# The second MLP product of the last two batches by seven products instead of eight

## The chip, the cores and the metric

The kernel runs on one core of a Trainium2 chip. The metric is the device time of one execution, in microseconds (us), as the median of several runs. A core has TensorE (PE in the profile; its weight loads are PEld), VectorE (DVE), ScalarE (ACT), GpSimd (POOL) and SyncE (SP, which here only issues transfers). Each engine takes its instructions in the order in which they are written and waits for the others by semaphores.

## The reference, cut to what matters

```python
# 8 batches, 12 heads, 448 positions, 64 columns per head
q_n, k_n = rmsnorm(q, g_q), rmsnorm(k, g_k)
attn = softmax(q_n @ k_n.T / 8) @ v                  # per batch and head
x = attn, heads side by side                         # 3584 tokens x 768
h = x @ w_in                                         # 3584 x 2048
g = maximum(h, 0) + alpha * minimum(h, 0)
out = g @ w_out                                      # 3584 x 768, float32
```

The change concerns the last line, for the last two of the eight batches (896 of the 3584 tokens).

## The kernel before, in words

Attention goes by groups of two head pairs; the MLP of a batch is laid beside the attention of the next batch, by a planner (L639 to L715) that gives each unit of MLP work a cost (`UP`, 1.13, and `DOWN`, 2.6) and deals the units out over the gaps between bursts of attention. The order on every engine is written out by this Python code; nothing reorders it later.

There are two kinds of MLP unit. `up` (L473) makes one 128-row slice of `g`, transposed, for one batch: six matmuls of 128x448 into a PSUM bank, then ScalarE writes `ah`, the product scaled by alpha (L494), then VectorE takes the maximum of product and `ah` into `gT` (L498). `gT` (L91) holds 16 such slices, f16, with 896 token columns: the even batch of a pair in columns 0 to 447, the odd one behind it. `down` (L500) makes 128 tokens by 384 of the 768 output columns: 16 matmuls of 128x384, one for each slice of `gT`, then VectorE copies the bank to `osb` (L520), and two transfers, issued by SP, write it out (L528). A pair of batches has seven token tiles `t` (0 to 6) and two column halves `oh`.

PSUM has eight banks: the pool `pss` has two tiles of two banks (tag `sc`, for attention scores), `psa` has one tile of two banks (tag `acc`), `psf` has two single banks (tag `mm`). `up` and `down` take a bank from `psf` in turn, or, with `spare` set, from `psa` (`bank`, L442). In the profile their tiles are `hT` and `op` in `psf`, `hTa` and `opa` in `psa`. A bank is free again when VectorE has read it (L498 or L520).

The end of the program is the list `rest` (L704 to L710, run at L917): the 16 `up` units of the last batch (7), with one of five `down` units left from before (token tile 0, half 1; tiles 1 and 2, both halves) ahead of every third `up`, and then the eight `down` units of token tiles 3 to 6. Every third entry of `rest` has `spare` set. The last `down` is done in two parts of 192 columns (L503), so that the copy and the transfers of the first part lie beside the second.

GpSimd computes squares (L155) and the scaled q and k (L179), issues the loads of v and of the weights, and adds up the softmax denominators of some head groups (`add_up`, L356). Its last work in the program is `add_up` for the last head group (23). `w_out_sb` (L90) holds the whole second weight matrix, f16, as 16 slices of 128 rows by 768 columns.

Of the kernel before, what the change touches and what calls it, by code (L numbers as in the profile page):

```python
# [9 lines left out]
FP32 = mybir.dt.float32  # L10
FP16 = mybir.dt.float16
# [10 lines left out]
def kernel(  # L22
# [12 lines left out]
    nc = tc.nc  # L35

    B, H, S, D = q.shape
    DM = H * D
    DF = moe_w_in.shape[1]
    J = S // 64  # L40
# [3 lines left out]
    NF = DF // 128  # L44
    OH = DM // 2
# [4 lines left out]
    EB = 3  # L50
# [5 lines left out]
    ld = ctx.enter_context(tc.tile_pool(name="ld", bufs=2))  # L56
    att = ctx.enter_context(tc.tile_pool(name="att", bufs=2))
    ffn = ctx.enter_context(tc.tile_pool(name="ffn", bufs=2))
    pss = ctx.enter_context(tc.tile_pool(name="pss", bufs=2, space=bass.MemoryType.PSUM))
    psa = ctx.enter_context(tc.tile_pool(name="psa", bufs=1, space=bass.MemoryType.PSUM))  # L60
    psf = ctx.enter_context(tc.tile_pool(name="psf", bufs=2, space=bass.MemoryType.PSUM))
# [7 lines left out]
    out4 = out.rearrange("(b p j) m -> b j p m", b=B, j=J)  # L69
# [16 lines left out]
    cols = cst.tile([128, NF + 2], FP32, name="cols", tag="cols")  # L86
# [3 lines left out]
    w_out_sb = cst.tile([128, NF, DM], FP16, name="w_out_sb", tag="w_out_sb")  # L90
    gT = cst.tile([128, NF, W], FP16, name="gT", tag="gT")  # L91
# [4 lines left out]
    nat, sqs, qs, ss_t, rr_t, qkT, vt, xT = {}, {}, {}, {}, {}, {}, {}, {}  # L96
# [220 lines left out]
    expT, rden, scs = {}, {}, {}  # L317

    def pre(ys):
        return len(ys) == 1 and ys[0] >= PRE and ys[0] % G == G - 1  # L320
# [179 lines left out]
    def down(b0, t, oh, jobs=(), spare=False):  # L500
# [24 lines left out]
        for c in range(parts):  # L525
            for half in range(2):
# [3 lines left out]
                    in_=o[ds(64 * half, 64), ts(c, PW)],  # L530
                )

    def spin(count, wide=True):

        ps = psf.tile([128, 512], FP32, name="spin", tag="mm")
        for _ in range(count):
            nc.tensor.matmul(
                out=ps[:, :S], lhsT=idle32[:, :128] if wide else ident,
                rhs=idle32 if wide else idle, start=True, stop=True,
            )  # L540
# [5 lines left out]
    den_at, av_at, split = {}, {}, {}  # L546
# [4 lines left out]
    m = 0  # L551
    while m < NG * J or steps:
        n = len(bursts)
# [20 lines left out]
        while len(bursts[n]) < limit and m < NG * J:  # L574
            y, j = divmod(m, J)
# [10 lines left out]
    NB = len(bursts)  # L586
# [17 lines left out]
    jobs = {}  # L604
    for y in range(G, NG):

        early = y < G + 2
        if early:
            n = turn_at[y - 1] + 1
        elif y == G + 2:  # L610
            n = den_at[G - 1]
        elif y == 2 * G:
            n = turn_at[y] - 4
        elif y % G == 1:
            n = den_at[y - 4] - 1 - pre((y - 2,))
        elif y % G:
            n = den_at[y - G] - pre((y - G,))
        else:
            n = av_at[y - 4]
# [22 lines left out]
    for b in range(B):  # L642
        ups = [(UP / 3 if b == 0 and ft < 4 else UP, up, (b, ft)) for ft in range(NF)]
        odd = b % 2
        new = [
            (DOWN, down, (b - odd, t, oh))
            for t in (range(3, J) if odd else range(3)) for oh in range(2)
        ]
# [16 lines left out]
    first = av_at[G - 1]  # L665
    gaps = [[] for _ in range(NB)]
    for b in range(B - 1):
        lo, hi = av_at[G * b + G - 1], av_at[G * b + 2 * G - 1]
        ups, old, new = (list(u) for u in periods[b])
        mlp = sum(u[0] for u in ups + old + new)  # L670
        stop = hi
# [5 lines left out]
        for n in range(lo, hi):  # L677
            clock += cost(n)
            free = True
            while ups or old or new:  # L680
                two = n in dens and pre(dens[n]) and len(gaps[n]) < 2
                if old and (not ups or (free or two) and (
                    wide(n) or len(old) > sum(wide(c) for c in range(n, hi))
                )):
                    u = old.pop(0)
                elif ups:
                    u = ups.pop(0)
                else:
                    u = new.pop(0)
# [12 lines left out]
                if n < hi - 1 and not short and clock + ahead > per * (n - lo + 1):  # L702
                    break
    ups, old, new = periods[B - 1]  # L704
    rest = []
    for n, u in enumerate(ups):
        if n % 3 == 0 and old:
            rest.append(old.pop(0)[1:])
        rest.append(u[1:])
    rest += [u[1:] for u in old + new]  # L710

    for n in range(1, NB):

# [7 lines left out]
    for n, g in enumerate((g_q, g_k)):  # L721
        for h in range(2):
            nc.gpsimd.dma_start(
                out=rows[NF + n : NF + n + 1, ds(64 * h, 64)], in_=g.unsqueeze(0)
            )
    load_qk(1, True)
    load_qk(2)

    spin(2)
    spin(17, False)  # L730
    ct = psf.tile([128, 512], FP32, name="ct", tag="mm")
    nc.tensor.transpose(ct[:, : NF + 2], rows, ident32[: NF + 2, : NF + 2])
# [4 lines left out]
    for h in range(2):  # L737
# [13 lines left out]
        out=gain, in0=cols[:, NF : NF + 1], in1=cols[:, NF + 1 : NF + 2]  # L751
# [30 lines left out]
    for n in range(NB):  # L782
# [6 lines left out]
        for t in first_tiles:  # L789
            if t == (0, J - 2):  # L790
                spin(1)
            elif t == (1, J - 3):
                spin(2, False)
            elif t == (1, J - 2):
                spin(1, False)
            elif t == (0, J - 1):
                turn_one(1, "q")
            elif t == (1, 0):
                turn_one(1, "k")
            elif t == (1, J - 1):  # L800
                turn(2)
            score(*t)
            if n == den_at[G - 1] - 1 and t == tiles[-1]:
                begin(0)
                begin(1)
            elif lead and t == tiles[0]:
                soft(*t)
                den(dens[n])
                attv(avs[n], 0, True, (log, invert))
            elif lead and t == tiles[1]:  # L810
                begin(2)
# [32 lines left out]
        if n in roots:  # L844
            y = roots[n]
# [41 lines left out]
        for k, (f, a) in enumerate(gaps[n]):  # L887
# [3 lines left out]
            else:  # L891
                f(*a, spare)
                done += 1
                if n in jobs and not (lead and done < 5) and (
                    n < av_at[2 * G - 1] or done % 2
                ):
                    g, c = jobs[n].pop(0)
# [3 lines left out]
                while late and done == late[0][0]:  # L901
                    _, g, c = late.pop(0)
# [11 lines left out]
                add_up(y, j)  # L914
        for f, a in jobs.pop(n, []) + post.get(n, []):
            f(*a)
    for k, (f, a) in enumerate(rest):  # L917
        f(*a, spare=k % 3 == 2)


# [28 lines left out]
```

## Time and profile before

| what | value |
|---|---|
| median of three runs | 428.4 us (428.13 to 429.29) |
| span of the profiled execution, first to last instruction | 425.6 us (no other time of it is given; the median lies 2.8 us above it) |
| TensorE busy | 413.7 us (97%) |
| ScalarE, GpSimd, VectorE busy | 275.3, 239.4 and 222.4 us |
| granted TensorE clock | 1.000 of full speed |
| last 16 `up` units begin | 372.40 us after the span's start |
| last matmul ends | 421.81 us |

A profile is one execution, recorded on the chip. The chain of waits follows the work that ended last back to what released each step. The timeline gives instructions in order of time: start and duration in us, engine, line, operation, output and inputs with their sizes, the count when several are merged, and in brackets the idle time before it with what ended it. Matmuls are pipelined; in the timeline their recorded durations overlap by some 0.16 us, in the chain of waits they do not.

### The profile page before, as it was taken

The page shows a single profiled execution, that of the slowest core. Times are in us where ns is not written, and L with a number is a line of the kernel's source. Part 1 is how long each engine was busy: PE and PEld are TensorE (multiplying, and loading weights), DVE is VectorE, ACT ScalarE, POOL GpSimd, SP SyncE. Part 2 cuts the span into 40 slices and gives each one's busy share as a digit, 9 for nine tenths or more (in the row PEclk, how much of TensorE's full clock was granted, in tenths as well). Part 3 has the DMA queues.
Part 4 walks back from the last instruction along what each step waited for, and adds up shares of the span by engine and source line. Part 5 has one row for each costly group of instructions (what it writes and reads, how often), then busy time and mean ns, then how long its engine had stood idle before and what let it go on. Part 6 is the DMA issues. An engine that isn't in the chain of part 4 may idle for free.

```text
span 425.6 us, 11138 instructions
## 1 busy us (share of the span) xinstructions
PE 413.7 (97%) x4755; PEld 216.5 (51%) x4755; DVE 222.4 (52%) x331; ACT 275.3 (65%) x384; POOL 239.4 (56%) x173
## 2 busy tenths in 40 slices
PE   7889999999999999999999999999999999999996
PEld 3344454544455454544555545554555445555554
DVE  4875964456454636636564545647453343343421
ACT  5898887778856686578846677668847575332200
POOL 6789993494997299373984479482973009000000
PEclk9999999999999999999999999999999999999999
DMA  8999999999538965568455963545333500111033
GB/s 199 242 240 224 204 195 204 204 195 238 117 73 131 210 102 126 85 158 168 97 104 109 187 148 106 105 103 126 62 55 85 104 2 22 39 37 39 18 76 75
DMA packets 68529, 53.36 MB, mean 125 GB/s; under 512 B 35568, under 2 KB 68480, under 8 KB 68480
## 3 DMA queue, kind: packets, MB, share of 16 engines
q1 hardware_dynamic: 53680, 39.73, 42.5%
q0 software_dynamic: 13984, 11.81, 18.5%
q10 hardware_dynamic: 816, 1.11, 1.0%
q8 instruction: 37, 0.61, 0.6%
q14 instruction: 12, 0.10, 0.1%
HBM read 45.62 MB, written 11.01 MB: 133 GB/s over the span
## 4 chain that ended last, share of the span: by engine, by line
PE 86%; ACT 5%; DVE 4%; POOL 2%; issue 1%; ACTq 1%; POOLq 0%
PE op L508 29%; PE hT L454 21%; PE hTa L454 9%; PE sc L329 8%; PE opa L508 6%; PE av L368 5%; PE dn L368 3%; ACT expT L343 2%; PE avb L368 2%; PE dnb L389 2%; ACT ah L494 2%; DVE gT L498 1%; POOL sq L155 1%; DVE ss L163 1%; ACTq L108 1%
## 5 line engine op out<-in xcount | busy, mean ns | idle before, releaser
L343 ACT ACTIVATE expT<-sc,expb 128x896 f16<-128x896 f32 x168 | 161.3, 1003 | 42.8 <-PE sc L329 42.6
L508 PE MATMUL op<-w_out_sb,gT 128*128 128x384 f16 (+1 forms) x752 | 125.8, 323 | 0.5 <-DVE gT L498 0.5
L508 PEld LDWEIGHTS <-gT 128*128 128x128 f16 x912 | 86.0, 98 | 64.7 <-issue 11.8
L454 PE MATMUL hT<-xT,w_in_sb 128*128 128x448 f16 x552 | 114.7, 353 | 0.8 <-DVE gT L498 0.5
L179 POOL TENSOR_TENSOR qs<-nat,rr 128x896 f16<-128x896 f32 x41 | 68.4, 1690 | 82.4 <-issue 45.6
L454 PEld LDWEIGHTS <-w_in_sb 128*128 128x128 f16 x768 | 73.2, 98 | 73.8 <-issue 9.4
L494 ACT ACTIVATE ah<-hT,cols 128x448 f16<-128x448 f32 x91 | 57.4, 632 | 46.5 <-PE hT L454 45.6
L498 DVE TENSOR_TENSOR gT<-hT,ah 128x448 f16<-128x448 f32 x92 | 57.3, 623 | 50.7 <-ACT ah L494 49.8
L155 POOL TENSOR_TENSOR sq<-nat 128x896 f32<-128x896 f32 (+1 forms) x47 | 75.5, 1625 | 7.9 <-DMA nat<-in_q_dram 7.3
L520 DVE COPY osb<-op 128x384 f32<-128x384 f32 (+1 forms) x47 | 25.7, 548 | 69.3 <-PE op L508 68.9
L329 PE MATMUL sc<-qT,kT 64*32 64x448 f16 (+1 forms) x1092 | 54.0, 356 | 4.4 <-ACT expT L343 2.2
L356 POOL TENSOR_TENSOR rden<-rden,expT 128x896 f32<-128x896 f32 x30 | 56.8, 1895 | 2.4
L163 DVE TENSOR_REDUCE ss<-sq 128x14 f32<-128x896 f32 (+1 forms) x48 | 48.9, 1039 | 1.9 <-POOL sq L155 1.8
L454 PE MATMUL hTa<-xT,w_in_sb 128*128 128x448 f16 x204 | 44.1, 352 | 0.0
L494 ACT ACTIVATE ah<-hTa,cols 128x448 f16<-128x448 f32 x34 | 21.6, 634 | 21.0 <-PE hTa L454 20.9
L329 PEld LDWEIGHTS <-kT 64*32 64x32 f16 (+1 forms) x1092 | 17.0, 93 | 35.7 <-issue 29.3
L498 DVE TENSOR_TENSOR gT<-hTa,ah 128x448 f16<-128x448 f32 x34 | 21.2, 624 | 19.6 <-ACT ah L494 18.9
L439 DVE TENSOR_TENSOR xT<-av,rden 128x896 f16<-128x896 f32 x16 | 17.5, 1091 | 21.5 <-ACT rden L410 15.4
L368 PEld LDWEIGHTS <-vt 64*32 64x32 f16 (+1 forms) x1260 | 21.4, 94 | 12.7 <-issue 2.5
L508 PE MATMUL opa<-w_out_sb,gT 128*128 128x384 f16 x160 | 27.7, 326 | 0.0
L368 PE MATMUL av<-expT,vt 64*32 64x448 f16 (+1 forms) x812 | 26.6, 349 | 0.0
L356 POOL TENSOR_TENSOR rden<-expT 128x896 f32<-128x896 f16 x6 | 11.3, 1878 | 20.9 <-ACT expT L343 20.9
(67 smaller groups left out, 215.8 us busy)
## 6 DMA issues: line engine op xcount, KB each, us to landing
out_dram<-osb SPq DMA_DIRECT2D x109, 96.0 KB, 2.2
nat<-in_q_dram SPq DMA_DIRECT2D x46, 224.0 KB, 4.3
nat<-in_k_dram SPq DMA_DIRECT2D x46, 224.0 KB, 4.8
vt<-in_v_dram POOLq DMA_DIRECT2D x16, 336.0 KB, 5.9
w_in_sb<-in_moe_w_in_dram POOLq DMA_DIRECT2D x12, 256.0 KB, 7.2
w_out_sb<-in_moe_w_out_dram POOLq DMA_DIRECT2D x4, 768.0 KB, 11.1
nat<-in_q_dram ACTq DMA_DIRECT2D x2, 224.0 KB, 4.3
nat<-in_k_dram ACTq DMA_DIRECT2D x2, 224.0 KB, 5.7
```

Source lines behind the costliest of these rows:

```text
L155: nc.gpsimd.tensor_mul(out=sqf[:, c], in0=src[:, c], in1=src[:, c])
L163: nc.vector.tensor_reduce(out=o[:, c], in_=sqs[y, nm][:, c], axis=AXIS_X, op=ALU.add)
L179: eng.tensor_mul(out=t.rearrange("p j h d -> p h j d"), in0=nat[y, nm], in1=rr_t[y][:, "qk".index(nm)].unsqueeze(3).broadcast_to((128, 2, ...
L329: nc.tensor.matmul(out=sc[ds(64 * g + m * c, m), par, :S].rearrange("p (j c) -> p j c", j=J), lhsT=kT[ds(64 * par, 64), j, g, ts(c, m)], r ...
L343: nc.scalar.activation(out=expT[y][:, j], in_=scs[y, j][:, :, :S], func=AF.Exp, scale=QK_SCALE, bias=expb[:, 0:1],)
L356: nc.gpsimd.tensor_add(out=s, in0=e[:, 0] if j == 1 else s, in1=e[:, j])
L368: nc.tensor.matmul(out=accs[g][ds(m * h, m), :S], lhsT=weights(g, y, par, ts(c, m), j), rhs=expT[y][ds(64 * g, 64), j, par, :], start=(j = ...
L454: nc.tensor.matmul(out=hT[:, :S], lhsT=w_in_sb[:, g * G + i, ts(ft, 128)], rhs=xT[b][:, g, i, :], start=(i == 0 and g == 0), stop=(i == G ...
L494: nc.scalar.activation(out=ah, in_=hT[:, :S], func=AF.Copy, scale=alpha_sb[:, ft : ft + 1])
L498: nc.vector.tensor_max(out=gT[:, ft, ds((b & 1) * S, S)], in0=hT[:, :S], in1=ah)
L508: nc.tensor.matmul(out=ops[c][:, :PW], lhsT=gT[:, ft, ts(t, 128)], rhs=w_out_sb[:, ft, ds(oh * OH + c * PW, PW)], start=(ft == 0), stop=(f ...
L520: nc.vector.tensor_copy(out=o[:, ts(c, PW)], in_=ops[c][:, :PW])
```

## The change

The four `down` units of tiles 1 and 2, and the eight of tiles 3 to 6, leave `rest`; only the one of tile 0 stays there, at its head. Behind `rest` come three calls of `quad`, for tiles (1, 2), (3, 4) and (5, 6). A `quad` makes both tiles and both column halves, four blocks of 128x384. The four blocks are products of a 2x2 block matrix of `gT` (two token tiles by two halves of the 16 slices) with a 2x2 block matrix of the weights (two halves of the slices by two column halves). By a Strassen scheme that takes seven block products, of eight matmuls each, in place of eight.

- `mix_weights` makes four sums of weight blocks, `tw[0]` to `tw[3]`, each 128x3072 f16, on GpSimd, in the order 0, 2, 1, 3. It stands at the end of step `NB - 2` of the main loop, behind the `add_up` of the last head group in GpSimd's order. The sums lie in buffers of `expT` that head groups 21 and 22 held.
- `mix` makes four sums of `gT` blocks, `gs`, each 128x1024 f16, on VectorE. For tiles 1 and 2 they are put into `rest`, one behind each of the entries 2, 5, 8 and 11; for the next `quad` they are put among the VectorE work of the one before.
- In a `quad` the seven products go into four PSUM banks (three of them twice; `quad` 1 and 3 use `pss`, `quad` 2 uses `psf` and `psa`). Three products per `quad` are copied or finished by ScalarE, four by VectorE additions, and one addition is on GpSimd; the outputs leave by `send`. In the last `quad` the last product is done in two parts of 192 columns.

```diff
+    halves = (slice(0, NF // 2), slice(NF // 2, NF))
+    tw, mixes = {}, {}
+    def mix_weights():
+        w = {(f, m): w_out_sb[:, halves[f], ts(m, OH)] for f in range(2) for m in range(2)}
+        for n in range(2):
+            t = att.tile([128, 2, NF // 2, OH], FP16, name="tw", tag="expT", bufs=EB)
+            tw[2 * n], tw[2 * n + 1] = t[:, 0], t[:, 1]
+        for n, x, y in (
+            (0, w[0, 1], w[0, 0]), (2, w[1, 1], w[0, 1]), (1, w[1, 1], tw[0]), (3, w[1, 0], tw[1])
+        ):
+            nc.gpsimd.tensor_sub(out=tw[n], in0=x, in1=y)
+    def mix(t0, eng):
+        a = {(n, f): gT[:, halves[f], ts(t0 + n, 128)] for n in range(2) for f in range(2)}
+        new = [
+            ld.tile([128, NF // 2, 128], FP16, name="gs", tag="nat", bufs=6) for _ in range(4)
+        ]
+        mixes[t0] = new
+        return [
+            lambda f=f, o=o, x=x, y=y: f(out=o, in0=x, in1=y)
+            for f, o, x, y in (
+                (eng.tensor_add, new[0], a[1, 0], a[1, 1]),
+                (eng.tensor_sub, new[1], new[0], a[0, 0]),
+                (eng.tensor_sub, new[2], a[0, 0], a[1, 0]),
+                (eng.tensor_sub, new[3], a[0, 1], new[1]),
+            )
+        ]
+    def send(b0, t, oh, o, c=slice(0, None), split=False):
...
+    def quad(b0, t0, wide, last=False, jobs=()):
+        a = {(n, f): gT[:, halves[f], ts(t0 + n, 128)] for n in range(2) for f in range(2)}
+        w = {(f, m): w_out_sb[:, halves[f], ts(m, OH)] for f in range(2) for m in range(2)}
+        s1, s2, s3, s4 = mixes[t0]
...
+        def product(bank, g, v, first, cols=slice(0, OH)):
+            for f in range(NF // 2):
+                nc.tensor.matmul(
+                    out=bank[:, cols], lhsT=g[:, f, :], rhs=v[:, f, cols],
+                    start=(first and f == 0), stop=(f == NF // 2 - 1),
+                    skip_group_check=True,
+                )
...
+        product(x, a[0, 0], w[0, 0], True)
+        m1 = part("m1")
+        nc.scalar.copy(out=m1, in_=x)
+        product(y, s2, tw[1], True)
+        u2 = part("u2")
+        nc.vector.tensor_add(out=u2, in0=y, in1=m1)
+        job()
+        product(p, s1, tw[0], True)
+        m5 = part("m5")
+        nc.scalar.copy(out=m5, in_=p)
+        product(q, s3, tw[2], True)
+        u3 = part("u3")
+        nc.vector.tensor_add(out=u3, in0=q, in1=u2)
+        job()
+        product(x, a[0, 1], w[1, 0], False)
+        o = ffn.tile([128, OH], FP32, name="osb", tag="osb", bufs=4)
+        nc.scalar.copy(out=o, in_=x)
+        send(b0, t0, 0, o)
+        nc.gpsimd.tensor_add(out=u3, in0=u3, in1=m5)
+        send(b0, t0 + 1, 1, u3)
+        job()
+        product(p, s4, w[1, 1], False)
+        o = ffn.tile([128, OH], FP32, name="osb", tag="osb", bufs=4)
+        nc.vector.tensor_add(out=o, in0=p, in1=u2)
+        send(b0, t0, 1, o)
+        job()
+        for c in (slice(0, OH // 2), slice(OH // 2, OH)) if last else (slice(0, OH),):
+            product(q, a[1, 1], tw[3], False, c)
+            nc.vector.tensor_add(out=u2[:, c], in0=q[:, c], in1=u2[:, c])
+            send(b0, t0 + 1, 0, u2, c, last)
...
     ups, old, new = periods[B - 1]
+    old = [u for u in old if u[2][1] == 0]
     rest = []
     for n, u in enumerate(ups):
         if n % 3 == 0 and old:
             rest.append(old.pop(0)[1:])
         rest.append(u[1:])
-    rest += [u[1:] for u in old + new]
...
+        if n == NB - 2:
+            mix_weights()
+    mixing = mix(1, nc.vector)
     for k, (f, a) in enumerate(rest):
         f(*a, spare=k % 3 == 2)
+        if k in (2, 5, 8, 11):
+            mixing[k // 3]()
+    nexts = {1: mix(3, nc.vector), 3: mix(5, nc.vector)}
+    for t in (1, 3, 5):
+        quad(B - 2, t, t != 3, t == 5, nexts.get(t, ()))
```

More of the change, by code (lines that the diff above doesn't have):

```diff
@@ new lines, in send, with job, part @@
+    def send(b0, t, oh, o, c=slice(0, None), split=False):
+        for half in range(2):
+            bb, j = divmod(2 * t + half, J)
+            dst = out4[b0 + bb, j, :, ts(oh, OH)]
+            (nc.scalar if split and half else nc.sync).dma_start(
+                out=dst[:, c], in_=o[ds(64 * half, 64), c]
+            )
[3 more added lines that the diff above has]
+        s1, s2, s3, s4 = mixes[t0]
+        if wide:
+            pairs = [pss.tile([128, 2, 512], FP32, name="oq", tag="sc") for _ in range(2)]
+            x, y, p, q = (t[:, n, :OH] for t in pairs for n in range(2))
+        else:
+            x = psf.tile([128, 512], FP32, name="oq", tag="mm")[:, :OH]
+            y = psf.tile([128, 512], FP32, name="oq", tag="mm")[:, :OH]
+            t = psa.tile([128, 2, 512], FP32, name="oqa", tag="acc")
+            p, q = t[:, 0, :OH], t[:, 1, :OH]
+        def product(bank, g, v, first, cols=slice(0, OH)):
[4 more added lines that the diff above has]
+                    skip_group_check=True,
+                )
+        jobs = iter(jobs)
+        def job():
+            for f in jobs:
+                f()
+                break
+        def part(name):
+            return ld.tile([128, OH], FP32, name=name, tag="sq", bufs=4)
+        product(x, a[0, 0], w[0, 0], True)
[28 more added lines that the diff above has]
+            send(b0, t0 + 1, 0, u2, c, last)
```

## The prediction, made before the changed kernel was run

> **What bounds the kernel now.** I read the page's summary first, then the end of the chain of waits, then the timeline of each engine over the last 75 us, since nothing ahead of 362 us moves: the built order of all engines is the same up to the new GpSimd instructions.
>
> ```profile
> span 425.6 us, 11138 instructions
> PE 413.7 (97%) x4755; PEld 216.5 (51%) x4755; DVE 222.4 (52%) x331; ACT 275.3 (65%) x384; POOL 239.4 (56%) x173
> PEclk9999999999999999999999999999999999999999
> ```
>
> TensorE is busy for 97% of the span at full clock. At the end it is the only bound:
>
> ```profile
> 413.96 2.60 PE opa L508 x16
> 416.56 5.25 PE op L508 x48
> 421.81 0.02 issue
> 421.84 0.36 DVE osb L520
> ```
>
> A `down` takes 2.60 us for 16 matmuls, 0.1626 us each; behind the last come a copy of 0.36 us and 3.4 us of transfer until 425.6. The stretch that changes is this (timeline of TensorE, then of VectorE, then of GpSimd):
>
> ```profile
> 372.24 1.30 PE L454 MATMUL hT<-xT,w_in_sb 128*128 128x448 f16 x6
> 373.37 1.30 PE L454 MATMUL hTa<-xT,w_in_sb 128*128 128x448 f16 x6
> 374.51 1.30 PE L454 MATMUL hT<-xT,w_in_sb 128*128 128x448 f16 x6
> ...
> 374.24 0.62 DVE L498 TENSOR_TENSOR gT<-hT,ah 128x448 f16<-128x448 f32 x1 [0.95 <-ACT ah L494]
> 375.37 0.63 DVE L498 TENSOR_TENSOR gT<-hTa,ah 128x448 f16<-128x448 f32 x1 [0.51 <-ACT ah L494]
> ...
> 352.43 9.79 POOL L356 TENSOR_TENSOR rden<-rden,expT 128x896 f32<-128x896 f32 x5
> ```
>
> An `up` takes 1.135 us (372.40, 373.54, 374.67 by the chain). VectorE releases its bank about 1.5 us after its last matmul, and three banks rotate, so 0.7 us of slack is left when `up` units follow each other. GpSimd is free from 362.22.
>
> One more view decides the case: what VectorE and GpSimd do to each other when both use SBUF. VectorE's in-place scaling of k takes 0.44 us at best and up to 1.90 us:
>
> ```profile
> 110.97 1.88 POOL L356 TENSOR_TENSOR rden<-expT 128x896 f32<-128x896 f16 x1
> ...
> 111.98 1.12 DVE L288 TENSOR_SCALAR kT<-kT,gain 128x896 f16<-128x896 f16 x1
> ...
> 122.69 3.46 POOL L155 TENSOR_TENSOR sq<-nat 128x896 f32<-128x896 f32 x2
> ...
> 122.93 1.69 DVE L288 TENSOR_SCALAR kT<-kT,gain 128x896 f16<-128x896 f16 x1
> ...
> 28.41 1.09 DVE L179 TENSOR_TENSOR qs<-nat,rr 128x896 f16<-128x896 f32 x1 [0.64 <-DMA nat<-in_q_dram]
> ...
> 29.26 1.79 POOL L179 TENSOR_TENSOR qs<-nat,rr 128x896 f16<-128x896 f32 x1
> ```
>
> The one at 111.98 ends at 113.10, 0.25 us after the GpSimd instruction that ran meanwhile (110.97 to 112.85). The one at 122.93 ends at 124.62, 0.25 us after the first of the two squares (122.69 to 124.37). It does not share; it waits for the whole GpSimd instruction, and then goes ahead of GpSimd's next, which loses 0.14 us (3.46 against 3.32 for an undisturbed pair). The last two rows are the only place where GpSimd starts under a VectorE instruction with two SBUF inputs: 1.79 us is the longest of 41 such instructions (median 1.69). So that form of VectorE instruction holds GpSimd up too. The new `gs` sums have this form. The maxima (L498) and the copies (L520) have at most one SBUF input beside PSUM, and keep 0.62 and 0.56 us whatever GpSimd does.
>
> [...]
>
> **Part by part.**
>
> *Removed and added on TensorE.* Twelve `down` units (192 matmuls' worth) become 3 x 7 x 8 = 168: 24 x 0.1626 = **-3.9 us**. Their drains lie beside the next product: per `quad` of 9.1 us, ScalarE gets three copies (nearest row: `ah`, 0.63) and VectorE four additions (0.6) and four sums; each bank has at least two products (2.6 us) before its reuse. So nothing there.
>
> *Sums of weights.* No row has 3072 elements. The nearest is the add of two f16 inputs, 1.878 us for 896. The squares give a fixed part: 0.925 for 448 and 1.69 for 896, so 0.16 fixed. Then (1.878 - 0.16) / 896 x 3072 + 0.16 = **6.05 us** each. Bounds: 5.41 by the squares' slope (1.708 ns), 6.50 with the add's 1.895 in proportion. All four go back to back from 362.3: `tw[0]` to 368.4, `tw[2]` to 374.4, `tw[1]` to 380.45, `tw[3]` to 386.5. The first `quad` needs `tw[1]` at 391.9, so the sums themselves are in time, by 11 us.
>
> *Sums of `gT`.* f16 in, f16 out, 1024 elements: 0.62 us for 896 (the f16 copies of q) gives 0.69; the f32 form (1.09 for 896) gives 1.2 as upper bound. Alone they cost nothing: 1.87 + 0.69 of VectorE in three `up` units of 3.41 us, and one delay of 0.69 against 0.7 us of slack.
>
> *The new wait.* They are not alone: GpSimd is busy without a gap from 362 to 386, and the first two `gs` stand there, with the maxima that free TensorE's banks queued behind them.
> 1. VectorE reaches `gs` 1 behind the second maximum, at 376.0. `tw[1]` (374.4 to 380.45) holds it. It ends at 380.45 + 0.5 = 380.95 (0.5: 0.69 less the 0.19 that the waiting instructions above had behind them).
> 2. The third maximum runs until 381.6. TensorE has done `up` 4 and 5 and stands from 378.07, since `up` 6 takes the bank of `up` 3. It goes on at 381.65: **3.6 us** lost.
> 3. `tw[3]` starts at 380.95 and ends at 387.0. The maxima of `up` 4 and 5 end at 382.8; `gs` 2 then waits until 387.0 and ends at 387.5; the maximum of `up` 6 at 388.1. TensorE does `up` 6 to 8 until 385.05 and stands until 388.2, for `up` 9: **3.15 us**.
> 4. `gs` 3 and 4 meet an idle GpSimd: nothing. Of a sum's length d the loss is about 4d - 17.5: 4.1 us at 5.41, 6.7 at 6.05, 8.5 at 6.50.
>
> So **+6.7 us**. Were the wait not there, no other work would be late: TensorE would run on.
>
> [...]
>
> *The end.* Last copy and transfers are as before, but four outputs (0.79 MB) leave in the last 2.5 us instead of two. In this kernel's tail they moved at 150 to 174 GB/s in busy slices and the queues went up to 242 GB/s early. Between 0 and 1.0 us; I take **+0.4**.
>
> **Sum**, on the profiled execution: 425.6 - 3.9 + 6.7 + 0.4 = 428.8 of span; the median lies 2.8 above the span, so **431.6 us**.
>
> **The rivals.**
>
> *No exclusion for this form.* VectorE's two-input sums could read beside GpSimd; the rows show only the one-input form waiting. Then the two stalls vanish: 428.4 - 3.9 + 0.4 = **424.9**, faster (424.4 to 425.5). For it: no VectorE instruction with two SBUF inputs starts under a GpSimd instruction in this trace. Against: the 1.79 row.
>
> *Short sums of weights.* With the squares' slope the stalls shrink to 4.1 us: 428.4 - 3.9 + 4.1 + 0.4 = **429.0**; below 5.65 us a sum it counts as no change or nearly. For it: squares of the same shape are shorter than adds. Against: both f16 rows are adds, and take 1.88.
>
> *GpSimd keeps the port.* If GpSimd's next instruction goes ahead of the waiting `gs` 1, VectorE waits until 386.5 once, and TensorE from 378.07 to 387.7: 9.6 us, **434.5**. At 218.65 a waiting instruction came just behind a GpSimd start and took 1.90 us, one instruction, not two; so unlikely.
>
> *The change doesn't do what it says*: excluded as far as the built order goes, which has 32 matmuls fewer (the split parts count double).
>
> **How the numbers follow.** Two stalls of 3 us or so each: 0.62 (430.0 to 434). Short sums: 0.11. No exclusion: 0.23. GpSimd first: 0.04. A measurement tells 0.3%, 1.3 us, from no change, so faster (under 427.1) 0.23, within 0.10, slower 0.67. The range must reach to the second case, 424.4, and takes the upper price of a sum and of the tail (8.5 and 1.0): 434.0, and 434.5 with the last rival. The likeliest case's own range is 429.0 to 434.0.
>
> **What would show it.** Right: `gs` 1 and 2 of some 4.5 us instead of 0.7, each ending 0.5 us behind a `tw`; TensorE idle before `up` 6 and `up` 9, for 3 us or so each, released by VectorE L498; a TensorE sum 3.9 us shorter; no stall in the `quad`s. Wrong: `gs` all of 0.7 us with `tw` beside them, or `tw` much off 6 us, or TensorE waiting inside a `quad`.

## The result, and the profile after

The changed kernel takes 437.29 us (median of 5 runs, 437.03 to 438.31) against 428.13 us in the same session: a ratio of 1.0221 (the two medians alone give 1.0214), with a 95% interval of 1.0202 to 1.0239. It is 9.2 us slower. The forecast was 431.6 us, with 434.5 us as the upper end: slower was right, the size was not.

The profiled execution took 438.31 us, the longest of the five; its span is 436.2 us, that of the other four 435.3. These lines of its page answer to those shown of before:

```profile
span 436.2 us, 11110 instructions
PE 412.1 (94%) x4723; PEld 213.5 (49%) x4723; DVE 238.8 (55%) x343; ACT 280.1 (64%) x393; POOL 267.5 (61%) x180
PE   7889999999999999999999999999999999778884
PEclk9899999999999999999999999999999999999999
```

TensorE has less to do (412.1 against 413.7 us) and is no longer busy without a break: from slice 35 on the digits are 7 and 8 (the 4 at the end holds the last transfer). The next two views show two different kinds of gap. First the part with the 16 `up` units, by the timeline of TensorE, VectorE and GpSimd:

```profile
377.46 1.30 PE L454 MATMUL hTa<-xT,w_in_sb 128*128 128x448 f16 x6
381.93 2.43 PE L454 MATMUL hT<-xT,w_in_sb 128*128 128x448 f16 x12 [3.17 <-DVE gT L498]
...
388.32 2.43 PE L454 MATMUL hT<-xT,w_in_sb 128*128 128x448 f16 x12 [2.83 <-DVE gT L498]
...
376.60 4.74 DVE L555 TENSOR_TENSOR gs<-gT 128x1024 f16<-128x1024 f16 x1
381.26 1.14 DVE L498 TENSOR_TENSOR gT<-hT,ah 128x448 f16<-128x448 f32 x2
382.33 0.61 DVE L498 TENSOR_TENSOR gT<-hTa,ah 128x448 f16<-128x448 f32 x1
382.86 4.88 DVE L555 TENSOR_TENSOR gs<-gs,gT 128x1024 f16<-128x1024 f16 x1
...
389.26 0.68 DVE L555 TENSOR_TENSOR gs<-gT 128x1024 f16<-128x1024 f16 x1
...
362.86 11.98 POOL L545 TENSOR_TENSOR tw<-w_out_sb 128x3072 f16<-128x3072 f16 x2
374.80 12.38 POOL L545 TENSOR_TENSOR tw<-w_out_sb,tw 128x3072 f16<-128x3072 f16 x2
```

This is the forecast wait. The first two `gs` take 4.74 and 4.88 us beside `tw`; the third, with GpSimd idle, takes 0.68. The maxima between them (one input in PSUM, one in SBUF) keep their 0.6 us with `tw[3]` beside them. TensorE stands twice, for 3.17 and 2.83 us, each time until a maximum behind a `gs` has released a bank.

Then the part with the seven products, first `quad`, with the two ScalarE copies and the VectorE addition that end the three gaps:

```profile
397.40 1.46 PE L588 MATMUL oq<-w_out_sb,gT 128*128 128x384 f16 x8
399.43 2.77 PE L588 MATMUL oq<-tw,gs 128*128 128x384 f16 x16 [0.57 <-ACT m L606]
402.78 1.46 PE L588 MATMUL oq<-tw,gs 128*128 128x384 f16 x8 [0.57 <-ACT m L613]
...
407.49 1.47 PE L588 MATMUL oq<-tw,gT 128*128 128x384 f16 x8 [0.65 <-DVE osb L627]
...
398.90 0.48 ACT L606 COPY m<-oq 128x384 f32<-128x384 f32 x1 [0.67 <-PE oq L588]
402.25 0.48 ACT L613 COPY m<-oq 128x384 f32<-128x384 f32 x1 [2.87 <-PE oq L588]
...
406.87 0.56 DVE L627 TENSOR_TENSOR osb<-oq,u 128x384 f32<-128x384 f32 x1
```

The second product goes into another bank than the first and takes nothing that the copy `m1` makes. Yet it starts only when that copy (398.90 to 399.38) has ended. The fourth product (402.78) starts in the same way behind the copy at 402.25, the last (407.49) behind the addition at 406.87. In this `quad` the banks `x` and `y` are two halves of one two-bank tile, and so are `p` and `q`; each of the three gaps lies where TensorE goes on to the second bank of a tile whose first bank is still being read.

From these views the 10.6 us between the two spans (436.2 and 425.6) come out as follows.

| stage | how it is read | us |
|---|---|---|
| up to the first of the 16 units | begins at 373.08 against 372.40 by the chains; not the change, see below | +0.7 |
| matmuls removed | 24 x 0.1626 | -3.9 |
| 16 `up` units | 373.08 to 397.56, 24.5 against 18.2 | +6.3 |
| three `quad`s | 397.56 to 431.68, 34.1 against 27.3 | +6.8 |
| last matmul to the end | 4.5 against 3.8 | +0.7 |

The first row belongs to this execution. Its granted clock is 0.83 between 10 and 20 us, where that of before is 1.00. By the timelines the units begin at 372.92 to 373.09 in three of the ten profiles of this case, this one among them, and at 372.03 to 372.25 in the other seven, five of which are of kernels with the same code up to there.

### The profile page after: what moved, and what is told of

Read it like the earlier page. It is cut to its first block, busy times and chain, and to the rows that moved or that the text cites. A ratio compares the mean times of both kernels' runs of the same rounds, so it can differ in the third digit from the quotient of the medians.

```text
span 436.2 us, 11110 instructions
## 1 busy us (share of the span) xinstructions
PE 412.1 (94%) x4723; PEld 213.5 (49%) x4723; DVE 238.8 (55%) x343; ACT 280.1 (64%) x393; POOL 267.5 (61%) x180
## 4 chain that ended last, share of the span: by engine, by line
PE 82%; DVE 8%; ACT 6%; issue 1%; POOL 1%; ACTq 1%; DVEq 0%; POOLq 0%
PE op L508 23%; PE hT L454 20%; PE sc L329 8%; PE hTa L454 8%; PE av L368 5%; PE oq L588 4%; PE opa L508 4%; DVE gs L555 3%; PE dn L368 3%; PE avb L368 2%; ACT expT L343 2%; DVE gT L498 2%; ACT ah L494 2%; PE dnb L389 2%; PE oqa L588 1%
## 5 line engine op out<-in xcount | busy, mean ns | idle before, releaser
L508 PE MATMUL op<-w_out_sb,gT 128*128 128x384 f16 x592 | 101.4, 326 | 0.5 <-DVE gT L498 0.5
L508 PEld LDWEIGHTS <-gT 128*128 128x128 f16 x704 | 66.1, 98 | 53.0 <-issue 11.8
L498 DVE TENSOR_TENSOR gT<-hT,ah 128x448 f16<-128x448 f32 x93 | 57.7, 623 | 46.9 <-ACT ah L494 46.1
L520 DVE COPY osb<-op 128x384 f32<-128x384 f32 x37 | 20.5, 556 | 55.0 <-PE op L508 54.6
L454 PE MATMUL hTa<-xT,w_in_sb 128*128 128x448 f16 x198 | 42.8, 352 | 0.0
L622 POOL TENSOR_TENSOR u<-u,m 128x384 f32<-128x384 f32 x3 | 3.7, 1249 | 37.1 <-DVE u L616 37.1
```

The source lines that it names most:

```text
L454: nc.tensor.matmul(out=hT[:, :S], lhsT=w_in_sb[:, g * G + i, ts(ft, 128)], rhs=xT[b][:, g, i, :], start=(i == 0 and g == 0), stop=(i == G ...
L498: nc.vector.tensor_max(out=gT[:, ft, ds((b & 1) * S, S)], in0=hT[:, :S], in1=ah)
L508: nc.tensor.matmul(out=ops[c][:, :PW], lhsT=gT[:, ft, ts(t, 128)], rhs=w_out_sb[:, ft, ds(oh * OH + c * PW, PW)], start=(ft == 0), stop=(f ...
```

## The experiments

All ratios are to the kernel before, in the same session and on the same chip; its medians are 428.1 us beside the change, 427.3 beside `no_weight_sums`, `sends` and the two kernels named `both_sends`, and 427.5 beside the others.

| kernel | us | ratio, 95% interval |
|---|---|---|
| the change | 437.29 | 1.0221 (1.0202 to 1.0239) |
| own_tiles | 431.98 | 1.0099 (1.0086 to 1.0112) |
| late_sums | 431.08 | 1.0080 (1.0067 to 1.0093) |
| half_weights | 432.00 | 1.0106 (1.0090 to 1.0123) |
| no_weight_sums | 431.06 | 1.0081 (1.0066 to 1.0096) |
| both | 426.13 | 0.9961 (0.9949 to 0.9974) |
| sends | 436.67 | 1.0223 (1.0206 to 1.0240) |
| both_sends | 424.05 | 0.9922 (0.9910 to 0.9934) |
| both_sends_whole | 424.44 | 0.9933 (0.9917 to 0.9949) |

**own_tiles: each bank from a tile of its own.**

```diff
-        if wide:
-            pairs = [pss.tile([128, 2, 512], FP32, name="oq", tag="sc") for _ in range(2)]
-            x, y, p, q = (t[:, n, :OH] for t in pairs for n in range(2))
...
+        x, p = (
+            pss.tile([128, 2, 512], FP32, name="oq", tag="sc")[:, 0, :OH] for _ in range(2)
+        )
+        y = psf.tile([128, 512], FP32, name="oqf", tag="mm")[:, :OH]
+        q = psa.tile([128, 2, 512], FP32, name="oqa", tag="acc")[:, 0, :OH]
```

> The changed kernel, with the four PSUM banks of each block product group taken from four tiles (the first bank of two tiles of two banks, one single bank, the first bank of the third two-bank tile) in place of two banks of one tile. Theory A: two banks of one tile are waited for as one, so that TensorE, before the second, fourth and last product, waits for the ScalarE copy or VectorE addition that reads the neighbouring bank; those nine waits cost 6.8 us in the profile (34.1 us from the first to the last matmul of this part against 27.3), of which only the one between the two halves of the last product (0.6) is a bank of its own: 437.3 - 6.2 = 431.1 us, and no TensorE idle time in this part but that one. Rival B: TensorE waits because the copies and additions themselves come too late: the waits stay, 437 us.

Measured: 431.98 us. The waits of TensorE from 370 us on, with the total, the number and the longest:

```profile
PE hT L454 <- DVE gT L498: 4.3, 2, 3.2
PE oqa L585 <- DVE u L629: 0.4, 1, 0.4
```

Of the nine waits in the `quad`s (three, two and three, and the one between the halves of the last product) eight are gone; the one between the halves, inside one bank, stays. The copies and additions take as long as before (0.48 and 0.56 us). So theory A holds: the waits were for neighbouring banks of a shared tile, not for late copies. The edit also takes the banks from other pools, but the built order names the sharing: in the changed kernel the first matmul of the first `quad`'s fourth product carries a wait for ScalarE, with separate tiles it carries none. It is a wait in the program, not one that the chip makes. From the first to the last matmul the `quad`s take 27.9 us (396.72 to 424.66) in place of 34.1, 6.2 less; the time fell by 1.22% (5.2 us). Of the difference 0.6 us was given back at the end (5.1 us behind the last matmul in place of 4.5), which is taken up below. (The two stalls among the `up` units sum to 4.3 us here and to 6.0 in the changed kernel, but the 16 units take 24.5 us in both: between the stalls twelve matmuls took 4.11 us in place of 2.43, see the account of the prediction.)

**late_sums, no_weight_sums and half_weights: what the first sums of `gT` wait for.** `late_sums` moves them behind GpSimd's work:

```diff
-        if k in (2, 5, 8, 11):
-            mixing[k // 3]()
+        if k > 12:
+            mixing[k - 13]()
```

> The changed kernel, with the first four VectorE sums of gT put behind entries 13 to 16 of the list in place of 2, 5, 8 and 11, when GpSimd has ended its sums of weights. Theory A: VectorE's two-input sums wait for the GpSimd instruction that runs, and the maxima behind them hold TensorE up, 6.3 us in all: each sum takes 0.7 us, TensorE has no idle time among the 16 first-product units, 437.3 - 6.0 = 431.3 us. Rival B: a sum between the maxima is by itself more than VectorE's slack; the stall moves along with the sums: 435 us or more.

`no_weight_sums` keeps their place and takes GpSimd's work away. It leaves out the sums of weights and puts plain weight blocks in their place, so its output is not the product:

```diff
-            tw[2 * n], tw[2 * n + 1] = t[:, 0], t[:, 1]
...
-            nc.gpsimd.tensor_sub(out=tw[n], in0=x, in1=y)
+        tw.update({0: w[0, 1], 2: w[1, 1], 1: w[1, 1], 3: w[1, 0]})
```

> The changed kernel with the four sums of weights on GpSimd left out (plain weight blocks of the same shape in their place), and the sums of gT on VectorE where they were, at entries 2, 5, 8 and 11. Theory A: without a GpSimd instruction beside them all four sums take 0.7 us and TensorE does not stand among the 16 units: the 6.3 us go, 431 us. Rival B: the place of the sums alone holds the maxima up: TensorE still waits before units 6 and 9, 435 us or more.

`half_weights` keeps both, and cuts each GpSimd instruction in two:

```diff
-            nc.gpsimd.tensor_sub(out=tw[n], in0=x, in1=y)
+            for c in (slice(0, 4), slice(4, 8)):
+                nc.gpsimd.tensor_sub(out=tw[n][:, c], in0=x[:, c], in1=y[:, c])
```

> The changed kernel, with each of the four GpSimd sums of weights in two instructions of half the size (about 3.1 us each). Theory A: VectorE waits for the rest of the one GpSimd instruction that runs, then goes first: the first two sums of gT take 2 to 2.5 us in place of 4.7 and 4.9, TensorE loses 1 to 2 us in place of 6.3: 432.5 us. Rival B: GpSimd keeps its access as long as it has work: the sums wait until GpSimd ends at 387, 440 us. Rival C: both share one rate, each is stretched: nothing changes, 437 us.

Measured: 431.08, 431.06 and 432.00 us. The VectorE sums in the timelines, first of `no_weight_sums`:

```profile
376.77 0.68 DVE L549 TENSOR_TENSOR gs<-gT 128x1024 f16<-128x1024 f16 x1
380.18 0.68 DVE L549 TENSOR_TENSOR gs<-gs,gT 128x1024 f16<-128x1024 f16 x1
```

and then of `half_weights`, with its GpSimd rows:

```profile
375.71 2.13 DVE L556 TENSOR_TENSOR gs<-gT 128x1024 f16<-128x1024 f16 x1
379.36 1.98 DVE L556 TENSOR_TENSOR gs<-gs,gT 128x1024 f16<-128x1024 f16 x1
383.24 1.60 DVE L556 TENSOR_TENSOR gs<-gT 128x1024 f16<-128x1024 f16 x1
386.73 1.60 DVE L556 TENSOR_TENSOR gs<-gT,gs 128x1024 f16<-128x1024 f16 x1
...
361.98 12.26 POOL L546 TENSOR_TENSOR tw<-w_out_sb 128x1536 f16<-128x1536 f16 x4
374.19 13.60 POOL L546 TENSOR_TENSOR tw<-w_out_sb,tw 128x1536 f16<-128x1536 f16 x4
```

At the same place among the maxima a sum takes 0.68 us without GpSimd, and TensorE has no wait among the 16 units, so the place alone costs nothing. With GpSimd instructions of 3.1 us in place of 6, the wait is at most the rest of one of them, and the waiting VectorE instruction goes in between: GpSimd's second group of four takes 13.60 us, 1.34 more than the first. TensorE's single wait among the `up` units is then 0.56 us, and the 16 units take 19.2 us against the 18.2 of 16 x 1.135. Sharing at a common rate would have changed nothing, and GpSimd keeping its access would have made it worse; both fall. So, in these runs, a VectorE sum with two SBUF inputs waits for the whole GpSimd instruction that is running, and then goes ahead of GpSimd's next. (The other direction is seen in the last section.)

**both: separate tiles and late sums.**

> Both edits together. Theory A: the two losses lie one behind the other and add up: 437.3 - 6.2 - 6.0 = 425.1 us, under the kernel before (428.1) by the 3.9 us of 24 matmuls less what the end gives back. Rival B: a new wait takes the place of those removed, as the sums then lie closer to their use: 428 us or more.

Measured: 426.13 us, 0.39% under the kernel before. The two losses add up: 1.22% and 1.41% alone, 2.60% together. TensorE goes from the first `up` (373.24, the 373.08 of its timeline and the overlap of 0.16) to the last matmul (419.35) in 46.1 us, against 49.4 before: 3.9 less, and 0.6 for the wait between the halves. But of this gain of 3.3 us only some 1.7 (0.39%) arrives; 1.4 go at the end. From VectorE's last addition (ended at 419.74) to the span's end there are 4.8 us, against 3.4 before. SP's timeline shows where they are (each row is two issues of one output):

```profile
416.65 1.12 SPq L568 DMA_DIRECT2D out_dram<-osb  x2
417.87 1.37 SPq L568 DMA_DIRECT2D out_dram<-u  x2
419.34 1.28 SPq L568 DMA_DIRECT2D out_dram<-osb  x2
420.71 1.19 SPq L568 DMA_DIRECT2D out_dram<-u  x2
```

An issue takes SP some 0.6 us. The four outputs become ready between 416.53 and 419.74, and SP is issuing all but without a break from 416.65 to 421.90 (eight issues, not the ten of the next expectation); its share of the first half of the last output, ready at 418.47, is not issued until 420.71. (A row of the last output is one issue of each half; ScalarE gives out the other two.)

**both_sends, both_sends_whole and sends: the end.** `send` has an argument that gives one of an output's two transfers to ScalarE; before, only the last output used it.

```diff
-        send(b0, t0, 0, o)
+        send(b0, t0, 0, o, split=last)
...
-        send(b0, t0 + 1, 1, u3)
+        send(b0, t0 + 1, 1, u3, split=last)
...
-        send(b0, t0, 1, o)
+        send(b0, t0, 1, o, split=last)
```

> The kernel with both edits (four tiles for the banks, late sums), and in the last group of products one of the two transfers of every output issued by ScalarE, in place of all but the last on SP. Theory A: behind the last matmul (419.35 us in the profile of both) the last VectorE addition ends at 419.74, but SP, which needs 0.6 us for each issue and has ten of them in five us, gives out its last one only at 421.9; the time of a transfer itself is unchanged (2.0 us). With the issues shared the end comes 1.2 us earlier: 424.9 us. Rival B: the transfers crowd each other, and the time from issue to landing grows instead: no change, 426 us.

Measured: 424.05 us, a ratio of 0.9922, 0.4% under `both`, with intervals that do not touch. SP's last issues now:

```profile
416.26 0.54 SPq L568 DMA_DIRECT2D out_dram<-u  x1
417.23 0.47 SPq L568 DMA_DIRECT2D out_dram<-osb  x1
417.80 1.48 SPq L568 DMA_DIRECT2D out_dram<-u  x2
```

The last issue begins within a half us of the last addition, and the end comes 3.3 us behind it (418.78 to 422.1), where `both` had 4.8. The time from issue to landing did not fall (2.1 and 2.3 us for the last halves, 1.9 and 2.2 in `both`), so the loss was the issuing, not crowded transfers.

`both_sends_whole` does the last product in one piece:

```diff
-        for c in (slice(0, OH // 2), slice(OH // 2, OH)) if last else (slice(0, OH),):
+        for c in (slice(0, OH),):
```

> As both_sends, with the last product done whole in place of in two halves of 192 columns. Theory A: TensorE waits 0.6 us between the halves, since the second goes into the bank that VectorE reads for the first; whole, the last addition takes 0.56 in place of 0.36 us and two issues fall away, so the end comes 0.3 to 0.5 us earlier: 424.5 us. Rival B: the first half's addition and transfer beside the second half are worth more than the wait: 425.3 us or more.

Measured: 424.44 us against 424.05, the intervals overlap, and the profiled spans are equal (422.1). The wait of 0.45 us between the halves and the larger last addition and transfer cancel. Theory A's 424.5 is met only because `both_sends` came in under its own forecast; the gain of 0.3 to 0.5 us over `both_sends` that A rests on is not there, and nor is B's loss.

`sends` has the shared issues alone, on the changed kernel:

> The changed kernel with the issues of the last group of products shared between SP and ScalarE, and nothing else. Theory A: its end, 4.5 us from the last matmul to the last instruction against 3.8 before, shrinks by up to 0.8 us: 436.4 us. Rival B: the banks' waits spread the outputs so that SP is not late there: 437.2 us.

Measured: a ratio of 1.0223 against 1.0221. In the profile its end is shorter (3.4 us from the last addition to the end, 4.1 in the changed kernel), but 0.7 us is inside the interval of the ratio: inconclusive. There the waits of the `quad`s spread the last four outputs over 4.0 us in place of the 3.2 of `both`, and SP has less to make up; that this is the reason was not tested apart.

## Why the prediction was wrong, point by point

- **Matmuls removed, -3.9 us: right.** `both` shows it, 3.3 net of the 0.6 of the halves.
- **Sums of weights, 6.05 us each: right.** 6.0 us measured for the first three (11.98 for the first pair) and 6.3 for the last, which starts while `gs` 1 still runs (380.87 against 381.34); that makes the second pair 12.38. The f16 add was the right row, not the squares.
- **Sums of `gT`, 0.69 us alone: right** (0.68). The slack beside them was put a little low: by the rows shown, VectorE releases a bank some 1.3 us behind its last matmul, not 1.5, which leaves 0.9 us, not 0.7. It changes nothing (`no_weight_sums` has no wait there).
- **The new wait, +6.7 us: right in mechanism and size.** 6.3 measured, at the two units named, released by the engine named; `late_sums`, `no_weight_sums` and `half_weights` confirm it. The rival that this form does not exclude GpSimd is refuted. In the trace of before the whole evidence for this form was a single row of 1.79 us against a median of 1.69, and that in the other direction (GpSimd held up by VectorE), beside the rows of another form. That so little carried was, as far as the trace goes, luck.
- **"Each bank has at least two products (2.6 us) before its reuse. So nothing there": this step failed**, and it is worth 6.8 us in the changed kernel's trace. It counted reuse by banks. The program's waits go by tiles, and two of a `quad`'s banks (in the second `quad`) or all four (in the others) share a tile with a neighbour. In the order x, y, p, q, x, p, q the second, the fourth and the last product go to one bank of a tile whose other bank the product just ended has filled, so no product lies between. Three times per `quad` (twice in the second) TensorE must wait out a readout of 0.48 or 0.56 us, and by the timeline stands for 0.57 to 0.65 us; `own_tiles` takes 6.2 us of this away. The other 0.6 is the wait between the halves of the last product, which do use one bank twice in a row. The waits stand in the built order, and nothing in the profile of before excluded them; the prediction itself had named TensorE waiting inside a `quad` as the sign that it was wrong. Without these waits its sum stands: `own_tiles` is 0.99% above the kernel before, and the forecast of 431.6 is 0.75% above 428.4.
- **The end, +0.4 us (0 to 1.0): too small, and for the wrong reason.** It was priced by the transfer rate. Where TensorE runs through (`both`) the end is 1.4 us longer, and SP's issuing sets it, as `both_sends` shows (3.3 us behind the last addition in place of 4.8). In the changed kernel it is 0.7 us longer, inside the bounds; that this is SP's issuing too is seen in the profile of `sends` only.
- **The granted clock behind the stalls**, for which the sum has no term, cost nothing. In the changed kernel's profile it is 1.00 from 372 to 420 us, across idle times of 3.17 and 2.83 us. `own_tiles` has the same code up to the `quad`s, and in its profile the clock falls there. Its rows, two of the timeline of TensorE and the clock from the page:

```profile
381.07 4.11 PE L454 MATMUL hT<-xT,w_in_sb 128*128 128x448 f16 x12 [3.16 <-DVE gT L498]
...
387.48 2.43 PE L454 MATMUL hT<-xT,w_in_sb 128*128 128x448 f16 x12 [1.16 <-DVE gT L498]
...
PEclk9999999999999999999999999999999999989999
```

  Behind the idle time of 3.16 us twelve matmuls take 4.11 us in place of 2.43; they lie in the slice of the page (376.1 to 386.8 us) whose digit is 8. The 1.7 us come out of the second stall, 1.16 us in place of 2.83, because the maximum that ends it waits for `gs` 2 and not for TensorE; the 16 units take 24.5 us in both profiles. In the changed kernel the first idle time was as long (3.17 us) and the clock stayed, so its length alone does not decide. Behind the second stall twelve matmuls take 2.43 us in both.

The forecast 431.6 plus the missed 6.8 would have been 438.4; the measured time is 437.3. Most of the 1.1 us between them is that the time lies 2.0 us above the span here (437.29 and 435.3), not 2.8 as in the prediction's base; the stalls came 0.4 us under their price and the end 0.3 over. What the range lacked was a price for TensorE waits in the new code, which it took as zero from both sides.

## What to carry to other kernels

When code with a new pattern of PSUM use is priced, read the waits of its built order instruction by instruction: in this program a wait follows the tile, not the bank, and TensorE that alternates between two banks of one tile pays the whole readout of the first (0.57 to 0.65 us each time here and 0.16 us of lost overlap, 6.2 us in all). When work is moved onto GpSimd, look for VectorE instructions with two SBUF inputs beside it (4.74 and 4.88 us here in place of 0.68), and for what stands behind those. Here moving the VectorE sums was worth as much as having no GpSimd work at all (431.08 and 431.06 us), and splitting the GpSimd instructions nearly as much (432.00). And when a bound engine finishes its outputs closer together, the queue that issues their transfers is the next thing to count (some 0.6 us an issue on SP): here the scheme of seven products took 3.9 us from TensorE, and brought 0.4% once the first two were mended and 0.8% (424.05 us) with all three.

## What the runs showed of the hardware that was not expected

The exclusion works in both directions, and is seen inside the `quad`s too. In the timeline of the changed kernel a GpSimd addition that starts while a `gs` runs is stretched, and the next `gs` waits for the rest of it:

```profile
404.80 0.68 DVE L555 TENSOR_TENSOR gs<-gs,gT 128x1024 f16<-128x1024 f16 x1
405.40 1.49 DVE L555 TENSOR_TENSOR gs<-gT 128x1024 f16<-128x1024 f16 x1
...
404.97 1.38 POOL L622 TENSOR_TENSOR u<-u,m 128x384 f32<-128x384 f32 x1 [17.78 <-DVE u L616]
...
427.07 1.00 POOL L622 TENSOR_TENSOR u<-u,m 128x384 f32<-128x384 f32 x1 [10.03 <-DVE u L616]
```

The addition takes 1.00 us in the last `quad`, which has no `gs` beside it, and 1.38 here; the `gs` behind takes 1.49 in place of 0.68. It costs TensorE nothing here: the wait ahead of the last product is 0.65 us with these sums and without them. The trace of before showed one direction for this form (the GpSimd row of 1.79 us against a median of 1.69); these rows show both.
